# Two batch pairs of a fused retention and adapter kernel: scores as causal 64x64 tiles with a state, or as whole 128x128 chunks

## The chip, the cores and the metric

The kernel runs on one core of one Trainium2 chip. Its time is the device time in microseconds, median of several runs. The engines of the core are TensorE (PE in the profile; PEld is its weight load), VectorE (DVE), ScalarE (ACT), GpSimd (POOL) and SyncE (SP), whose queue issues most DMA transfers. Each engine takes its instructions in program order and waits on semaphores that other engines raise.

## The reference

Eight batches, eight heads, 576 positions, head dimension 64. First a retention layer without softmax, then a mixture of low-rank adapters on its output:

```python
scores = scale * np.matmul(q, k.transpose(0, 1, 3, 2))
gamma = 1.0 - 2.0 ** (-5.0 - np.arange(H, dtype=np.float32))
Dmat = np.where(rel >= 0, gamma[:, None, None] ** rel[None, :, :], 0.0)   # rel = i - j
x = np.matmul(scores * Dmat[None], v)          # B H S D, then to rows of B*S by H*D
...
logits = x @ w_gate                            # 8 experts, the best 2 chosen
w = softmax over the two chosen logits
out = x + sum over the chosen e of w_e * (x @ A[e]) @ B[e]     # rank 16
```

The decay gamma^(i-j) splits into gamma^i on the query and gamma^(-j) on the key, so that a causal 0/1 mask is all that is left to apply to the scores. Since there is no softmax, all earlier positions can be summed into one 64x64 matrix of keys by values for each head, a state; the product of a query with that state stands for all of them.

## The kernel before

The work is cut into 18 units. Units 0 to 15 are (chunk c, batch pair bp): 128 positions of two batches with eight heads each; units 0 to 3 are the first chunk (c = 0) of the four pairs, units 4 to 7 the second, and so on. Units 16 and 17 hold the last 64 positions of four batches each. All work of a unit goes through the same stages:

- `load` brings q, k, v by the SP queue (L182). `scale_` (L210) multiplies keys or queries by their powers of gamma.
- `stage_T` (L234) transposes keys or queries on TensorE with the 64x64 identity; `evict_T` (L285) copies the result from PSUM to `kT` or `qT`.
- scores, sums and products, in one of two forms, below.
- `stage_Z` (L511, called by `logits` and `logits_half`): x times AW, which holds the rank-16 adapters A of all experts (128 columns) and the gate (8 columns). `routing_1` to `routing_4` choose the experts: a ScalarE copy of the logits (`zs`), VectorE maxima (`choose`), ScalarE sigmoid (`routing_3`), GpSimd weighting (`routing_4`).
- `back` (`stage_B`, L574) transposes x back to rows in PSUM, `small` (`stage_P`, `evict_z`) transposes the weighted 128 values and ScalarE copies them to `zT`; `output` (`stage_Y`, `evict_o`) adds zT times B into the same PSUM banks, and ScalarE copies them out to `osb`. `store` writes to memory.

Units 0 to 3 use the whole-chunk form: `first_S` (L426) scores 128 keys against 128 queries of a head pair with unscaled transposes and multiplies them by the full decay table `dec` on VectorE (L442, four instructions a unit); `first_U` (L463) sums keys by values of all 128 positions to the state `SP[bp]` (copy L478); `first_X` (L480) multiplies 128 scores by v. Only the keys are scaled, after their transposes, for the sums.

Units 4 and up use the tiled form, in halves t = 0, 1 of 64 positions: `stage_S` (L316) scores only the two diagonal 64x64 tiles of each head; `masks` (L337) applies the triangle on VectorE (four instructions of 64 partitions), writing into `qT` or the tile `x2`; `stage_U` (L349) sums each half by itself, `stage_A` (L385) adds the first half's sums to the state (`sm`) and then the second's (`SP`). Half t = 0 takes `SP` as its state and half t = 1 takes `sm`. `put_state` (L368) copies a state to the 64 partitions of the v tile that the half does not fill; `shift_q` (L308) copies queries to the facing 64 partitions of `x2`. So `stage_X` (L394) gets scores times v and queries times state in one contraction over 128 rows. From unit 4 on the queries of a full unit are loaded with even and odd positions apart.

PSUM has eight banks, named by tags s0, s1, x0, x1, u0, u1, o0, o1; a stage that writes a bank waits for the last reader of the one before it.

The order of the work is written out by hand. L663 to L735 are units 0 and 1; L946 to L1004 finish unit 1 and take units 2 and 3 and the beginning of unit 4, each interleaved with the routing of earlier units; L1006 on is the rest, in a loop from unit 5. The adapters A arrive as `arow` (32 rows of 2048), are reordered by two GpSimd copies (`sort_A`, L640), transposed by 16 TensorE instructions and copied to AW by VectorE (`place_A`, L645). Transfers of later units start by a count of products: `product` (L158) adds 4 for a float32 product and 2 for a transpose or a 16-bit one, and at each 255th count `feed` lets the SP queue issue the next half round of loads, and, in the last rounds, of stores (`transfers`, L744).

Of the kernel before, what the change touches and what calls it, by code (L numbers as in the profile page):

```python
# [18 lines left out]
def kernel(  # L19
# [49 lines left out]
    pack_np = np.concatenate([id64_np, gk_np[:, 0], tri_np], axis=1).astype(np.float32)  # L69
# [38 lines left out]
    tri = pack[:, 64 + H : NPK]  # L108
# [3 lines left out]
    def factor(w, c):  # L112
        if c == 0:
            return pack[:, 64 : 64 + H]
        return (gk2 if w == "k" else gq2)[:, c - 1, :]
# [16 lines left out]
    def first_chunk(u):  # L132
        return u < NP
# [15 lines left out]
    def block(u, t):  # L149
        return nt(u, "v")[:, t]  # L150
# [31 lines left out]
    def load(u, w, parts=(0, 1), at=None):  # L182
        if u >= NU:
            return
        c, bp = units[u]
        s0 = 128 * c
        if c == NFULL:
            for t in parts:
                hf = slice(64 * t, 64 * t + 64)
                dst = block(u, t)[hf] if w == "v" else nt(u, w)[hf]  # L190
                move(dst, rows(w, 4 * bp + 2 * t, 2, s0, 64), at)
        elif w == "v" and c == 0:
            move(block(u, 0), rows(w, 2 * bp, 2, s0, 128), at)
        elif w == "v":
            for t in parts:
                hf = slice(64 * t, 64 * t + 64)
                move(block(u, t)[hf], rows(w, 2 * bp, 2, s0 + 64 * t, 64), at)
        elif w == "q" and paired(u):
            for b in parts:
                move(  # L200
                    nt(u, w)[64 * b : 64 * b + 64].rearrange("p (h e) d -> p h (e d)", e=2),
                    q[2 * bp + b, :, s0 : s0 + 128, :].rearrange(
                        "h (p e) d -> p h (e d)", e=2
                    ),
                    at,
                )
        else:
            move(nt(u, w), rows(w, 2 * bp, 2, s0, 128), at)
# [76 lines left out]
    def evict_T(u, w, b=None, engines=(nc.scalar, nc.scalar)):  # L285
        tl = transposed(u, w)
        for r, eng in enumerate(engines):
            copy = eng.copy if eng is nc.scalar else eng.tensor_copy
            if w == "k" and first_chunk(u):
# [47 lines left out]
    def masks(u, b=None, order=((0, 0), (1, 0), (0, 1), (1, 1))):  # L337
# [47 lines left out]
    def stage_A(u):  # L385
# [3 lines left out]
        nc.vector.tensor_tensor(out=sm, in0=pu[0], in1=SP[bp], op=ALU.add)  # L389
# [4 lines left out]
    def stage_X(u, tag="x", bs=(0, 1)):  # L394
        px = st[u].setdefault("px", {})
        for b in bs:
            px[b] = pp.tile([128, HP, 2, ST], FP32, tag=f"{tag}{b}", name=f"px{b}")
# [65 lines left out]
    def first_U(u, tag="u0"):  # L463
# [14 lines left out]
        nc.vector.tensor_copy(out=SP[units[u][1]], in_=pu)  # L478
# [161 lines left out]
    def sort_A():  # L640
        rows_ = arow.rearrange("p (d r) -> p r d", r=R)
        for r in (slice(0, R // 2), slice(R // 2, R)):
            nc.gpsimd.tensor_copy(out=asort[:, r], in_=rows_[:, r])

    def place_A(tag):  # L645
        pa = pp.tile([128, R, E * HP], FP32, tag=tag, name="pa")
        for r in range(R):
            product(
                pa[:, r, :], lhsT=asort[:, r, :], rhs=id64[64 : 64 + E * HP, 0 : E * HP],
                is_transpose=True, start=True, stop=True,  # L650
            )
        nc.vector.tensor_copy(  # L652
            out=AW[:, :, 0:ER].rearrange("p t (e r) -> p t e r", e=E),
            in_=pa.rearrange("p r (e t) -> p t e r", t=HP),
        )
# [24 lines left out]
    asort = atile[64 : 64 + E * HP].rearrange("p (r d) -> p r d", r=R)  # L680
# [15 lines left out]
    share = (nc.vector, nc.scalar)  # L696

# [37 lines left out]
    sort_A()  # L735
# [63 lines left out]
    def sums(u):  # L799
        if is_full(u):  # L800
            stage_U(u)
            if units[u][0] > 0:
                stage_A(u)

    def put(u):
        if is_full(u):
            src = st[u]["sm"] if units[u][0] > 0 else st[u]["pu"][0]
            put_state(u, 1, src, nc.scalar)
# [149 lines left out]
    scale_(2, "k", pool2)  # L958
# [124 lines left out]
```

## Time and profile before

| | |
|---|---|
| median of 3 runs | 177.18 us (176.99 to 177.76) |
| the profiled execution: its time | 178.47 us |
| its span, first to last instruction | 176.6 us |
| mean granted TensorE clock | 0.991 |
| read and written in memory | 29.11 MB, 9.44 MB |
| first scores of unit 1 | 16.17 us |
| first logits (unit 0) | 22.73 us |
| scores of unit 4 | 46.60 us |
| last store issued | 172.0 us |

The chain of waits goes back from the last instruction to what released each. The groups give, for each line, engine and shape, the busy time, the mean of one and the idle time before; L159 is the helper that issues every TensorE instruction, so its groups are told apart by tile: `pf_s`, `pf_u`, `pf_x` are scores, sums and products of whole chunks, `ps_s`, `pu`, `px` those of tiles, `pt_k` and `pt_q` the transposes, `pz` and `pzh` the logits, `po` the way back and the output, `pzt` the small transpose, `pa` the adapters. A float32 product is two instructions.

### The profile page before, as it was taken

What the parts mean: (1) busy time and instruction counts of PE and PEld (TensorE: products, weight loads), DVE (VectorE), ACT (ScalarE), POOL (GpSimd) and SP (SyncE); (2) the same over time, 40 slices, a digit from 0 to 9 for tenths busy, and PEclk for the clock granted to TensorE, in tenths of its full rate; (3) what the DMA queues carried; (4) which work ended last, traced back from release to release, by engine and by line L of the source; (5) the groups of instructions that cost most, each with busy time, mean ns of one, the idle gap of its engine ahead of it and who ended that gap; (6) DMA issues with size and microseconds to landing.
All of it is one profiled execution on the core that took longest, in us unless ns stands there. A gap on an engine that the chain in (4) does not pass through costs nothing.

```text
span 176.6 us, 9664 instructions
## 1 busy us (share of the span) xinstructions
PE 167.9 (95%) x4306; PEld 151.7 (86%) x4306; DVE 112.4 (64%) x221; ACT 105.8 (60%) x242; POOL 113.0 (64%) x162
## 2 busy tenths in 40 slices
PE   7999999999999999999999999999999999999950
PEld 7789988888998999999999998989898889898930
DVE  0375626552766978787889878777776765847060
ACT  3225225744677595858677676768586765584730
POOL 1228608697498477959497959696975797930250
PEclk9999999999999999999999999999999999999996
DMA  6989999999964778787878787959679899999994
GB/s 153 270 190 230 243 238 236 246 249 225 249 148 126 173 191 182 187 186 190 196 188 198 187 194 178 227 143 220 164 164 223 183 247 255 377 390 346 348 358 144
DMA packets 105929, 39.04 MB, mean 221 GB/s; under 512 B 88664, under 2 KB 101336, under 8 KB 105856
## 3 DMA queue, kind: packets, MB, share of 16 engines
q1 hardware_dynamic: 105360, 37.64, 83.9%
q8 instruction: 34, 0.56, 1.3%
q0 software_dynamic: 288, 0.52, 1.3%
q10 hardware_dynamic: 240, 0.25, 0.5%
q14 instruction: 7, 0.06, 0.1%
HBM read 29.11 MB, written 9.44 MB: 218 GB/s over the span
## 4 chain that ended last, share of the span: by engine, by line
PE 87%; DVE 5%; ACT 2%; issue 2%; POOL 1%; POOLq 0%; ACTq 0%
PE px L159 17%; PE pz L159 16%; PE ps_s L159 9%; PE po L159 9%; PE pu L159 6%; PE pt_k L159 6%; PE pt_q L159 5%; PE pf_s L159 4%; PE pf_x L159 4%; PE pf L159 3%; PE pf_u L159 2%; DVE qT L347 2%; DVE x L347 2%; PE pzh L159 1%; PE pzt L159 1%
## 5 line engine op out<-in xcount | busy, mean ns | idle before, releaser
L226 POOL TENSOR_TENSOR k<-k,pack 128x512 f32<-128x512 f32 x36 | 38.5, 1087 | 27.6 <-DMA k<-in_k_dram 18.4
L159 PE MATMUL pz<-AW,xT 128*128 128x136 f32 x256 | 34.2, 286 | 0.1
L159 PEld LDWEIGHTS pz<-AW,xT 128*128 128x128 f32 x256 | 30.8, 190 | 1.4 <-DVE AW L652 0.3
L159 PE MATMUL px<-x,v 128*64 128x64 f32 x448 | 30.0, 224 | 0.6 <-issue 0.5
L159 PE MATMUL px<-qT,v 128*64 128x64 f32 x448 | 29.6, 224 | 0.1
L159 PEld LDWEIGHTS px<-x,v 128*64 128x64 f32 x448 | 27.6, 138 | 2.4 <-issue 0.8
L159 PEld LDWEIGHTS px<-qT,v 128*64 128x64 f32 x448 | 27.2, 138 | 0.0
L347 DVE TENSOR_TENSOR x<-ps_s,pack 64x512 f32<-64x512 f32 x28 | 19.3, 689 | 10.8 <-PE ps_s L159 10.4
L216 POOL TENSOR_TENSOR qs<-q,pack 128x512 f32<-128x512 f32 x24 | 24.5, 1043 | 1.8 <-DMA q<-in_q_dram 1.0
L529 ACT COPY zs<-pz 128x272 f32<-128x272 f32 x16 | 6.2, 386 | 25.3 <-PE pz L159 24.0
L374 POOL COPY v<-SP 64x512 f32<-64x512 f32 x32 | 19.5, 611 | 1.6
L347 DVE TENSOR_TENSOR qT<-ps_s,pack 64x512 f32<-64x512 f32 x28 | 19.3, 689 | 0.8
L615 ACT COPY osb<-po 128x512 f32<-128x512 f32 x32 | 17.1, 591 | 2.7 <-PE po L159 2.7
L310 DVE COPY x<-qT 64x512 f32<-64x512 f32 x14 | 10.1, 724 | 13.0 <-ACT qT L294 9.1
L159 PEld LDWEIGHTS ps_s<-qT,kT 64*64 64x64 f32 x896 | 14.7, 134 | 3.3 <-issue 1.3
L159 PE MATMUL ps_s<-qT,kT 64*64 64x64 f32 x896 | 16.9, 221 | 0.1
L554 ACT ACTIVATE sg<-zs,ns 128x8 f32<-128x8 f32 x34 | 8.4, 293 | 13.5 <-DVE ge L544 12.8
L564 POOL TENSOR_TENSOR cm<-ge,sg 128x16 f32<-128x16 f32 x17 | 5.7, 337 | 16.5 <-ACT sg L554 16.5
L374 ACT COPY v<-sm 64x512 f32<-64x512 f32 x24 | 14.9, 620 | 0.1
L299 ACT COPY kT<-pt_k 128x512 f32<-128x512 f32 x28 | 14.8, 579 | 0.2 <-PE pt_k L159 0.2
L566 POOL TENSOR_TENSOR zc<-zs,cm 128x128 f16<-128x128 f32 x34 | 13.6, 421 | 1.3
L159 PE MATMUL pu<-v,k 64*64 64x64 f32 x768 | 14.2, 221 | 0.1
(89 smaller groups left out, 302.0 us busy)
## 6 DMA issues: line engine op xcount, KB each, us to landing
q<-in_q_dram SPq DMA_DIRECT2D x32, 256.0 KB, 4.4
out_dram<-osb SPq DMA_DIRECT2D x32, 256.0 KB, 4.3
k<-in_k_dram SPq DMA_DIRECT2D x14, 512.0 KB, 5.3
v<-in_v_dram SPq DMA_DIRECT2D x28, 256.0 KB, 4.1
k<-in_k_dram SPq DMA_DIRECT2D x8, 256.0 KB, 5.0
v<-in_v_dram SPq DMA_DIRECT2D x4, 512.0 KB, 5.7
q<-in_q_dram SPq DMA_DIRECT2D x2, 512.0 KB, 6.8
arow<-in_moe_A_dram SPq DMA_DIRECT2D x1, 256.0 KB, 4.6
```

The lines of the kernel that those rows point to most:

```text
L159: mm = nc.tensor.matmul(out, lhsT=lhsT, rhs=rhs, is_transpose=is_transpose, **kw)
L216: engines[b].tensor_tensor(out=qs[:, :, 4 * b : 4 * b + 4, :].rearrange("p e h d -> p h e d"), in0=tl[:, b * H : b * H + H, :].rearrange(" ...
L226: engines[b].tensor_tensor(out=tl[:, b * H : b * H + H, :], in0=tl[:, b * H : b * H + H, :], in1=factor(w, c).unsqueeze(2).broadcast_to((1 ...
L299: copy(out=tl[:, r], in_=st[u]["p" + w][r])
L310: eng.tensor_copy(out=x2[64:128, 0, b], in_=qT[0:64, 0, b])
L347: nc.vector.tensor_tensor(out=out, in0=in0, in1=m, op=ALU.mult)
L374: copy(out=dst[:, :, :, ho, :], in_=src[64 * ho : 64 * ho + 64])
L529: nc.scalar.copy(out=zs, in_=s["pz"])
L554: nc.scalar.activation(out=sg[:, b, :], in_=s["zs"][:, b, ER : ER + E], func=AFT.Sigmoid, bias=s["ns"][:, b : b + 1], scale=2.0,)
L564: nc.gpsimd.tensor_tensor(out=cm, in0=s["ge"], in1=s["sg"], op=ALU.mult)
L566: nc.gpsimd.tensor_tensor(out=zc[:, b, :].rearrange("p (e r) -> p e r", e=E), in0=s["zs"][:, b, 0:ER].rearrange("p (e r) -> p e r", e=E), ...
L615: copy(out=s["osb"][:, :, :, ho, :], in_=s["po"][ho])
```

## The change

Units 2 and 3 take the tiled form; only units 0 and 1 stay whole chunks. Having no positions before them, they have no state for t = 0: `stateful(u)` is false for them. Then `stage_X` contracts only 64 rows for t = 0, `stage_A` copies the first half's sums instead of adding, and `masks` does both tiles of t = 0 first. Keys and queries are scaled before the transposes (`mixed` gives one batch to GpSimd and one to VectorE), the table `pack` gets the queries' factors, and v of units 2 and 3 is loaded in two halves. `stage_X` can be called for one half t alone. The adapters A are transposed by four VectorE instructions of 32 partitions each, straight into AW; `sort_A` is gone. The sums of unit 1 are copied by ScalarE. The order of L946 to L1004 is written anew.

```diff
-    pack_np = np.concatenate([id64_np, gk_np[:, 0], tri_np], axis=1).astype(np.float32)
+    pack_np = np.concatenate(
+        [id64_np, gk_np[:, 0], gq_np[:, 0], tri_np], axis=1
+    ).astype(np.float32)
...
-    def first_chunk(u):
-        return u < NP
+    def whole_chunk(u):
+        return u < 2
+
+    def stateful(u):
+        return units[u][0] > 0
...
-        elif w == "v" and c == 0:
+        elif w == "v" and whole_chunk(u):
...
-    def masks(u, b=None, order=((0, 0), (1, 0), (0, 1), (1, 1))):
+    def masks(u, b=None):
+        order = ((0, 0), (1, 0), (0, 1), (1, 1)) if stateful(u) else (
+            (0, 0), (0, 1), (1, 0), (1, 1)
+        )
...
-        nc.vector.tensor_tensor(out=sm, in0=pu[0], in1=SP[bp], op=ALU.add)
+        if stateful(u):
+            nc.vector.tensor_tensor(out=sm, in0=pu[0], in1=SP[bp], op=ALU.add)
+        else:
+            nc.vector.tensor_copy(out=sm, in_=pu[0])
...
-    def stage_X(u, tag="x", bs=(0, 1)):
+    def stage_X(u, tag="x", bs=(0, 1), ts=(0, 1)):
...
-                for t in range(2):
+                for t in ts:
+                    kp = slice(0, 128) if t or stateful(u) else slice(0, 64)
...
-                            lhsT=block(u, t)[:, b * H + 2 * hp + ho, :],
-                            rhs=facing(u, t, ho)[:, b, hp, :],
+                            lhsT=block(u, t)[kp, b * H + 2 * hp + ho, :],
+                            rhs=facing(u, t, ho)[kp, b, hp, :],
...
-    def first_U(u, tag="u0"):
+    def first_U(u, tag="u0", engine=nc.vector):
...
+    def place_A(groups):
+        rows_ = arow.rearrange("p (g d r) -> p g r d", g=4, r=R)
+        for g in groups:
+            nc.vector.transpose(
+                out=AW[32 * g : 32 * g + 32, :, 0:ER].rearrange("p t (e r) -> p r e t", e=E),
+                in_=rows_[:, g],
+            )
...
+    mixed = (nc.gpsimd, nc.vector)
...
+    place_A(range(1))
     first_S(1, 0, "s")
     first_S(1, 1, "o")
-    first_U(1)
+    first_U(1, engine=nc.scalar)
     first_X(1, "x")
-    place_A("u1")
+    place_A(range(1, 4))
     back(0)
+    scale_(2, "k", mixed)
     logits(0, "u1")
+    scale_(2, "q", mixed)
     choose(0)
     routing_3(0)
     routing_4(0)
     stage_T(2, "k", tag="s")
     evict_T(2, "k")
-    scale_(2, "k", pool2)
     stage_Z(1, "u0", (0,))
     stage_T(2, "q", tag="x")
     evict_T(2, "q", engines=share)
     stage_Z(1, "u0", (1,))
+    shift_q(2, nc.vector)
     routing_1(1)
-    small(0, "u1")
     choose(1)
     routing_3(1)
-    first_S(2, 0, "s")
-    first_S(2, 1, "x")
+    scores(2)
+    small(0, "x1")
     output(0)
-    routing_4(1)
-    first_U(2)
+    sums(2)
+    scale_(3, "k", pool2)
+    scale_(3, "q", pool2)
+    put(2)
+    back(1)
+    stage_X(2, ts=(0,))
     stage_T(3, "k", tag="s")
-    evict_T(3, "k")
-    scale_(3, "k", pool2)
-    first_X(2, "x", (0,))
+    evict_T(3, "k", engines=share)
+    stage_X(2, ts=(1,))
+    evict_x(2)
     stage_T(3, "q", tag="u")
     evict_T(3, "q", engines=share)
-    first_X(2, "x", (1,))
-    back(1)
-    small(1, "x0")
-    first_S(3, 0, "s")
-    first_S(3, 1, "x")
+    routing_4(1)
+    small(1, "s0")
+    shift_q(3, nc.vector)
+    logits_half(2, 0, "x0")
+    scores(3)
     output(1)
-    scale_(4, "k", pool2)
-    scale_(4, "q", pool2)
-    first_state(4)
-    for w in "kq":
-        scale_(5, w, pool2)
-    first_U(3)
+    for u in (4, 5):
+        for w in "kq":
+            scale_(u, w, pool2)
+        if u == 4:
+            first_state(4)
+    sums(3)
     seen["round"] = 3
-    logits_half(2, 0, "u1")
-    first_X(3, "x", (0,))
+    put(3)
+    logits_half(2, 1, "x1")
     stage_T(4, "k", tag="o")
     evict_T(4, "k")
-    sums(4)
+    stage_X(3, ts=(0,))
     stage_T(4, "q", tag="s")
     evict_T(4, "q")
-    first_X(3, "x", (1,))
-    logits_half(2, 1, "o0")
-    shift_q(4, nc.vector)
     choose(2)
     routing_3(2)
+    stage_X(3, ts=(1,))
+    evict_x(3)
+    shift_q(4, nc.vector)
+    sums(4)
     put(4)
     routing_4(2)
```

More of the change, by code (lines that the diff above doesn't have):

```diff
@@ L107 @@
     id64 = pack[:, 0:64]
-    tri = pack[:, 64 + H : NPK]
+    tri = pack[:, 64 + 2 * H : NPK]
     fac = cpool.tile([128, 128 + HP * 128], FP32, tag="fac", name="fac", align_bytes=256)
@@ L113, in factor @@
         if c == 0:
-            return pack[:, 64 : 64 + H]
+            return pack[:, 64 : 64 + H] if w == "k" else pack[:, 64 + H : 64 + 2 * H]
         return (gk2 if w == "k" else gq2)[:, c - 1, :]
@@ L288, in evict_T @@
             copy = eng.copy if eng is nc.scalar else eng.tensor_copy
-            if w == "k" and first_chunk(u):
+            if w == "k" and whole_chunk(u):
                 bs = slice(0, 2) if b is None else slice(b, b + 1)
@@ L477, in first_U @@
                     )
-        nc.vector.tensor_copy(out=SP[units[u][1]], in_=pu)
+        copy = engine.copy if engine is nc.scalar else engine.tensor_copy
+        copy(out=SP[units[u][1]], in_=pu)
     def first_X(u, tag, bs=(0, 1)):
@@ L638, in store @@
                     )
[L640 to L650, printed above, removed]
-            )
[L652 to L655, printed above, removed]
+    def place_A(groups):
[4 more added lines that the diff above has]
+                in_=rows_[:, g],
+            )
     def load_batch(u, w, b):
@@ L679 @@
     arow = atile[0 : E * HP]
-    asort = atile[64 : 64 + E * HP].rearrange("p (r d) -> p r d", r=R)
     nc.sync.dma_start(out=arow, in_=moe_A.rearrange("e (t p) r -> (e t) (p r)", t=HP))
@@ L734 @@
     evict_T(1, "q", 1, share)
-    sort_A()
     def prepare(t):
@@ L801, in sums @@
             stage_U(u)
-            if units[u][0] > 0:
-                stage_A(u)
+            stage_A(u)
     def put(u):
         if is_full(u):
-            src = st[u]["sm"] if units[u][0] > 0 else st[u]["pu"][0]
-            put_state(u, 1, src, nc.scalar)
+            put_state(u, 1, st[u]["sm"] if stateful(u) else st[u]["pu"][0], nc.scalar)
     def products(u):
```

3 lines of the change are left out of this document (2 added, 1 removed).

## The prediction, made before the changed kernel ran

> **What bounds the kernel now.** I read the page's engine sums first, then the sums by stretch.
>
> ```profile
> PE 167.9 (95%) x4306; PEld 151.7 (86%) x4306; DVE 112.4 (64%) x221; ACT 105.8 (60%) x242; POOL 113.0 (64%) x162
> 28.50:46.60 18.10, 18.10 (x366) 15.80 (x369) 10.15 (x20) 9.95 (x21) 13.35 (x17) 1.00 1.04 237
> ```
>
> TensorE is busy 95% of the span, and in the stretch that the change rewrites (second row, columns PE, PEld, DVE, ACT, POOL) it is busy 18.10 of 18.10 us; VectorE has 8 us to spare there, ScalarE too. So a matmul removed here is time gained, unless TensorE then waits for an engine that was hidden. The chain of waits gives the price of each stage (start, us, what; x counts instructions, two for a float32 product).
>
> ```profile
> 20.84 1.12 PE pa L159 x16
> 21.99 0.70 DVE AW L652
> 22.73 2.12 PE pz L159 x16
> ...
> 26.62 0.65 PE pt_q L159 x16
> 27.27 1.12 PE pz L159 x8
> 28.39 0.11 PE pzt L159 x2
> 28.50 1.99 PE pf_s L159 x32
> 30.49 0.54 PE po L159 x4
> 31.03 1.08 PE pf_u L159 x32
> ...
> 32.76 1.02 PE pf_x L159 x16
> ...
> 46.60 1.09 PE ps_s L159 x64
> ...
> 51.10 1.08 PE px L159 x32
> 52.18 1.09 PE pu L159 x64
> ```
>
> The rows from 46.60 on are the tiled form, which units 4 to 15 use already. I measure the change from logits(0) (22.73) to the scores of unit 4 (46.60), because both kernels run the same stages between these two, though in another order, and the same program after.
>
> **Term 1, TensorE work.** A whole-chunk unit costs 1.99 + 1.08 + 2 x 1.02 = 5.11 us (scores, sums, products), a tiled one 1.09 + 1.09 + 2 x 1.08 = 4.34. Two units: **-1.54 us**. The products of t=0 contract 64 rows, not 128. No row has that form; at best it runs like the sums (1.09 for 64 instructions, so 0.55 for a half), at worst like px (1.08). Both outputs of a t=0 pair use rows 0 to 63, so half of the array has no work, where the sums alternate between both halves: I take 1.08, the bound being 1.1 us lower for two units.
>
> **Term 2, the weights A.** Removed: two strided GpSimd copies (sort_A), 16 PE transposes (1.12) and one VectorE copy. Added: four VectorE transposes of 32x512.
>
> ```profile
> 17.16 2.48 DVE L442 TENSOR_TENSOR sc<-pf_s,dec 128x512 f32<-128x512 f32 x4 [0.52 <-PE pf_s L159]
> L389 DVE TENSOR_TENSOR sm<-pu,SP 128x512 f32<-128x512 f32 x12 | 8.3, 691 | 5.3 <-PE pu L159 4.9
> L643 POOL COPY arow<-arow x2: 1954/1962/1971, 16.6 to 18.5; 32x1024 f32<-32x1024 f32 x2
> L374 POOL COPY v<-SP 64x512 f32<-64x512 f32 x32 | 19.5, 611 | 1.6
> ```
>
> A has landed by 16.6, where GpSimd begins to copy it. VectorE is free from 17.16 - 0.52 = 16.64; the first transpose goes there, then the four masks of unit 1 (2.48), then the other three. logits(0) needs all four: 16.64 + 2.48 + 4 tau. A VectorE pass over 512 elements takes 0.69 us (L389), the lower end. The transposes read with a step of 16 floats; GpSimd's copy with that step took 1962/1024 = 1.92 ns an element against 611/512 = 1.19 without, a factor of 1.6, which makes 1.11 the upper end. VectorE's copy of A out of PSUM, which reads with a step too, took 0.70 (21.99 above), so I take tau = 0.8, nearer to the lower end: logits(0) at 22.35, **-0.38 us** (-0.8 to +0.85). TensorE gets there at 20.84 + 0.65 (back(0): 16 transposes, as in T) and waits. [...]
>
> The sums of unit 1 are copied by ScalarE instead of VectorE; ScalarE has nothing to do before the products of unit 1 end, so this costs nothing, and VectorE gets its three transposes 0.7 us sooner.
>
> **Term 3, a new wait at output(0).** TensorE now runs T(2,q), Z(1) half, scores(2), small(0), output(0). output(0) needs the ScalarE copy zT, which stands behind the sigmoid of unit 1, which needs choose(1) on VectorE, which stands behind the new shift_q(2).
>
> ```profile
> 27.30 0.69 DVE L299 COPY qT<-pt_q 128x512 f32<-128x512 f32 x1 [1.47 <-PE pt_q L159]
> 27.48 2.04 POOL L226 TENSOR_TENSOR k<-k,pack 128x512 f32<-128x512 f32 x2
> 28.71 0.38 ACT L508 COPY zT<-pzt 128x256 f16<-128x256 f16 x1
> 28.84 0.24 DVE L539 MAX8 m<-zs 128x8 f32<-128x8 f32 x2 [0.86 <-ACT zs L529]
> 29.63 0.49 ACT L554 ACTIVATE sg<-zs,ns 128x8 f32<-128x8 f32 x2 [0.55 <-DVE ge L544]
> L310 DVE COPY x<-qT x14: 420/619/1305, 45.6 to 157.6; 64x512 f32<-64x512 f32 x14
> L311 DVE COPY x<-qT x14: 421/1170/1171, 46.0 to 158.1; 64x512 f32<-64x512 f32 x14
> ```
>
> Today zT (28.71) precedes the sigmoid (29.63). Now, from the end of T(2,q): qT copy 0.69, two shift copies, choose 28.84 to 29.63 = 0.79, sigmoid 0.49, zT 0.38, five handovers of some 0.04: 2.55 without the shifts. Their rows give shortest, median and longest in ns: together 0.84 at least and 2.48 at most; GpSimd scales keys just then (27.48 today, unit 3's keys in the same place after), so I take a mean of 1.6. In all 4.15; TensorE covers 1.12 + 1.09 + 0.11 = 2.32. **Stall 1.8 us** (1.1 to 2.7). Behind output(0) TensorE holds sums(2), back(1) and products(2), all late by it. [...]
>
> The next wait is near: products(2) of t=1 need the four masks, the new sm copy and put(2).
>
> ```profile
> L347 DVE TENSOR_TENSOR x<-ps_s,pack 64x512 f32<-64x512 f32 x28 | 19.3, 689 | 10.8 <-PE ps_s L159 10.4
> L374 ACT COPY v<-sm 64x512 f32<-64x512 f32 x24 | 14.9, 620 | 0.1
> 46.63 0.27 ACT L788 COPY zs<-pzh 128x136 f32<-128x136 f32 x1 [0.53 <-PE pzh L159]
> ```
>
> From the end of choose(1): 4 x 0.69 + 0.69 + 2 x 0.62 + 0.1 = 4.8; TensorE, from the same point: 1.0 to output(0) (sigmoid 0.49, zT 0.38, handovers), then 0.54 + 1.09 + 0.65 + 1.08 + 0.65 = 4.0, in all 5.0. It fits by 0.2: nothing added.
>
> **Term 4, a new wait in products(3).** The second batch of t=0 writes bank x1, which logits_half(2, 1) filled and ScalarE empties behind put(3). From the end of scores(3): masks 2.76, sm 0.69, put 1.24, zs 0.27, handovers 0.15: 5.1. TensorE covers output(1) 0.54, sums(3) 1.09, logits_half 1.12, T(4,k) 0.65, one batch of t=0 0.54: 3.94. **Stall 1.2 us** (1.15 to 1.5, the more if shift_q(3) still holds VectorE). Behind put(3) on ScalarE also stand the copies of kT(4) and qT(4); scores(4) come some 3.3 us after the stall and need 0.3 + 4 x 0.6 of them, so they are covered.
>
> **Edits at nothing.** Keys and queries of units 2 and 3 are scaled before their transposes; four query instructions are new.
>
> ```profile
> 15.66 0.50 SPq L174 DMA_DIRECT2D k<-in_k_dram  x1
> 23.35 2.21 SPq L174 DMA_DIRECT2D q<-in_q_dram  x1
> k<-in_k_dram SPq DMA_DIRECT2D x1, 512.0 KB, 5.5
> q<-in_q_dram SPq DMA_DIRECT2D x1, 512.0 KB, 6.8
> ```
>
> k(2) lands at 15.66 + 5.5 = 21.2. Half goes to GpSimd (1.04, half of the 2.04 above), half to VectorE after the transposes: ready by 23.4, and T(2,k) comes at 24.4. Without that cover the wait would be 1.0. The latest is q(3): 23.35 + 6.8 = 30.15, scaled at 32.2, with routing_4(1) queued behind it until 33.2; small(1) needs that at about 36. k(4) is not in yet then, so no later scaling is pushed. v(2) and v(3) are two DMAs each instead of one, of the same bytes on the same queue. The shared copy of kT(3) on VectorE (0.69) lies after sm, where TensorE has products.
>
> **Term 5, the stores.** Loads and stores start at every 255th count of products (4 for a float32 product, 2 else). Each tiled unit counts 384 instead of 192, the lost transposes 32: +352, one block and 97. All later transfers start 97 counts earlier in the program; the last stores start in the scores of unit 17 instead of back(15), earlier by the logits between them (2.12) and parts of the two, some 3 us.
>
> ```profile
> 164.00:165.00 1.00, 1.00 (x41) 1.00 (x38) 0.00 (x0) 1.00 (x3) 0.76 (x2) 1.00 0.50 182
> DMA to landing us min/median/max: 3.2/3.4/3.5
> pack<-c_pack ACTq DMA_DIRECT2D x1, 100.0 KB, 2.2
> ```
>
> The DMA engines are half idle at 164 (share 0.50, the last column but one), and the final stores (second line, shortest, median and longest us of 128 KB stores) land 3.4 us after issue, behind that queue; a transfer of like size at the very start, with little ahead of it, lands after 2.2 (last row). Starting the stores earlier fills the gap (0.5) and shortens the queue: the gain is between 0 and 3.4 - 2.2 = 1.2. I take **-0.7**, the gap and a little.
>
> **Sum.** -1.54 - 0.38 + 1.8 + 1.2 - 0.7 = +0.4 us. The profiled execution took 178.47 (span 176.6): 178.9. The median of the runs shown is 1.29 lower: 177.18 + 0.4 = **177.6**.
>
> **Rivals.** A measurement of this kernel can tell 0.5%, 0.9 us: under 176.3 is faster, over 178.1 slower.
> - A, slower: the strided transposes. At 1.11 each, logits(0) starts 4 x 0.31 = 1.2 later than forecast: 178.8. It decides from 0.92 each on. For it GpSimd's factor, against it VectorE's 0.70 for today's copy. 0.18. [...]
> - B, slower: the last data, not the store queue, sets the end; term 5 falls away: 178.3. For it: the last stores are issued within 0.5 us of their data. 0.14.
> - C, slower: the change does not shorten TensorE's work, because switching between half and whole contraction costs what the tiles save: 179.1. Against it: units 4 and up pay 1.09 in mixed company. 0.05.
> [...]
> - The forecast, no change that can be told: 0.40.
>
> So faster 0.23, same 0.40, slower 0.37. Likeliest case alone: 176.3 to 178.1. With the bounds of tau (+1.2), the port and the t=0 form, 8 in 10: 176.0 to 179.2.
>
> **What would show it.** Scores and sums of units 2 and 3 at 1.09 us each; logits(0) near 22.35 and the transposes' mean near 0.8 us; TensorE idle some 1.8 us before output(0), ended by ScalarE's zT, and 1.2 us in products(3), ended by zs; scores(4) near 47.7; DMA share near 1 at the end until the last store. It is wrong if there is no idle time at these two places, if the idle time stands elsewhere (put(2) first), or if the tail keeps its length.

## The result, and the profile after

The changed kernel takes 182.88 us, the median of 6 runs (181.81 to 184.29); the kernel before took 177.74 beside it (176.99 to 178.25). The ratio is 1.0301, 95% interval 1.026 to 1.0341: slower, outside the predicted range. The profiled execution took 183.72 us with a span of 181.9, against 178.47 and 176.6 before, so +5.3 us of span are to be explained. (Lines have moved: the product helper is L164, the transposes of A L657.)

The page's engine sums, the row of granted clock in 40 slices, and the instruction queue of its list of DMA queues:

```profile
PE 167.7 (92%) x4482; PEld 151.4 (83%) x4482; DVE 111.7 (61%) x232; ACT 108.6 (60%) x246; POOL 111.1 (61%) x162
PEclk9999999699999999999999999999999999999997
q8 instruction: 35, 0.57, 1.3%
```

TensorE is busy as long as before (167.7 against 167.9 us), though it does less: one slice ran at a lower clock. The rest of the 5.3 us is time in which it stands still. The chain of waits (start, us, what) between the logits of unit 0 and the scores of unit 4, at the places that the prediction named:

```profile
17.93 2.45 DVE sc L455 x4
20.41 1.15 DVE AW L657
21.58 1.15 DVE AW L657
22.73 1.13 DVE AW L657
23.91 2.12 PE pz L164 x16
...
28.48 0.69 DVE qT L304
29.20 0.72 DVE x L315
29.94 1.17 DVE x L316
31.12 0.25 DVE m L553 x2
31.39 0.64 DVE ns L554
32.03 0.10 DVE ge L558
32.12 0.49 ACT sg L568 x2
32.62 0.27 ACT zT L522
...
33.63 1.92 PE pu L164 x64
...
36.59 1.15 PE px L164 x32
...
38.39 1.08 PE px L164 x32
...
47.08 0.28 ACT zs L793
...
50.90 1.14 PE ps_s L164 x64
```

Logits(0) start at 23.91 instead of 22.73 (+1.18), because each transpose of A takes 1.13 to 1.15 us (and the first of the four, ahead of these rows, began at 16.94, when A had landed). From there to the scores of unit 4 it is 26.99 us instead of 23.87 (+3.12). TensorE's timeline (start, us, instruction; in brackets the idle time before it and what ended it) shows the two waits:

```profile
32.93 0.70 PE L164 MATMUL po<-Bcat,zT 128*128 128x256 f16 x4 [2.05 <-ACT zT L522]
47.41 0.27 PE L164 MATMUL px<-x,v 64*64 64x64 f32 x1 [0.98 <-ACT zs L793]
```

Behind the first of them the sums of unit 2 take 1.92 us instead of 1.09. The view by stretches (window, length, busy time and count of PE, PEld, DVE, ACT, POOL, then clock, DMA share, GB/s) says why:

```profile
33.00:34.00 1.00, 1.00 (x20) 0.67 (x24) 0.97 (x3) 0.65 (x2) 0.92 (x4) 0.66 1.21 274
34.00:36.00 2.00, 2.00 (x70) 1.88 (x64) 1.04 (x3) 0.43 (x1) 0.04 (x1) 0.50 0.63 158
36.00:37.00 1.00, 1.00 (x24) 0.88 (x22) 0.90 (x2) 0.65 (x2) 0.68 (x1) 0.64 1.21 310
```

TensorE was granted half its clock from 33.3 to 36.7 us (a mean of 0.66 over the first microsecond means half for 0.68 of it, 0.64 over the last for 0.72). The chain's rows give what that cost: output(0) 0.70 instead of 0.54, the sums 1.92 instead of 1.09, the way back 1.05 for 0.65, the first products 1.15 for 1.08: 1.46 us. So the stretch adds up: 2.05 + 0.98 + 1.46 - 1.54 (the work saved) = 2.95 of the 3.12. The six runs' mean clocks fit: 181.81 us at 0.995, 182.80 to 183.72 at 0.985 to 0.987, 184.29 at 0.976.

From the scores of unit 4 to the end it is 131.0 us instead of 130.0. The end itself is shorter, as the landing of the last stores (shortest, median and longest us, row of the tile `oe`) and the chain show:

```profile
DMA to landing us min/median/max: 2.7/2.9/3.0
```

```profile
172.38 1.00 PE pze L164 x8
```

The same row of the chain before:

```profile
166.08 1.00 PE pze L159 x8
```

From the last logits to the end of the span it is 181.9 - 172.38 = 9.52 us; before it was 176.6 - 166.08 = 10.52. So 1.0 is gained there and 2.0 is lost between. The view of waits (who waits, for whom; us in total, times, longest) names a loss that no term of the prediction has, "issue", time in which TensorE waits for nothing that the profile shows:

```profile
PE po L164 <- ACT zT L522: 2.1, 1, 2.1
PE px L164 <- issue: 1.1, 2, 0.8
PE ps_s L164 <- issue: 0.6, 1, 0.6
PE pz L164 <- issue: 0.5, 1, 0.5
```

The kernel before has one row of that kind, 0.5 us. These halts are what most of the experiments are about.

### The profile page after: what moved, and what is told of

Its sections match the earlier page's. It is cut to its first block, busy times and chain, and to the rows that moved or that the text cites. A ratio compares the mean times of both kernels' runs of the same rounds, so it can differ in the third digit from the quotient of the medians.

```text
span 181.9 us, 10038 instructions
## 1 busy us (share of the span) xinstructions
PE 167.7 (92%) x4482; PEld 151.4 (83%) x4482; DVE 111.7 (61%) x232; ACT 108.6 (60%) x246; POOL 111.1 (61%) x162
## 4 chain that ended last, share of the span: by engine, by line
PE 83%; DVE 9%; issue 3%; ACT 2%; POOL 1%; POOLq 0%; ACTq 0%; DVEq 0%
PE px L164 18%; PE pz L164 18%; PE po L164 9%; PE ps_s L164 9%; PE pu L164 8%; PE pt_k L164 6%; PE pt_q L164 6%; PE pf L164 3%; PE pf_s L164 2%; DVE AW L657 2%; DVE sc L455 1%; PE pf_x L164 1%; DVE x L316 1%; PE pzt L164 1%; DVE x L315 1%
## 5 line engine op out<-in xcount | busy, mean ns | idle before, releaser
L164 PE MATMUL px<-x,v 128*64 128x64 f32 (+1 forms) x512 | 35.1, 224 | 2.1 <-issue 1.1
L164 PE MATMUL pz<-AW,xT 128*128 128x136 f32 x256 | 34.7, 287 | 2.2 <-DVE AW L657 1.7
L164 PEld LDWEIGHTS px<-x,v 128*64 128x64 f32 (+1 forms) x512 | 31.9, 138 | 4.0 <-issue 1.4
L164 PE MATMUL px<-qT,v 128*64 128x64 f32 (+1 forms) x512 | 34.6, 224 | 0.0
L355 DVE TENSOR_TENSOR x<-ps_s,pack 64x512 f32<-64x512 f32 x32 | 22.0, 688 | 20.0 <-PE ps_s L164 19.7
L164 PEld LDWEIGHTS pz<-AW,xT 128*128 128x128 f32 x256 | 30.9, 190 | 3.8 <-DVE AW L657 1.9
L164 PEld LDWEIGHTS px<-qT,v 128*64 128x64 f32 (+1 forms) x512 | 31.5, 138 | 0.3
L355 DVE TENSOR_TENSOR qT<-ps_s,pack 64x512 f32<-64x512 f32 x32 | 22.0, 688 | 0.9
L164 PEld LDWEIGHTS ps_s<-qT,kT 64*64 64x64 f32 x1024 | 17.1, 134 | 4.0 <-issue 2.3
L164 PE MATMUL ps_s<-qT,kT 64*64 64x64 f32 x1024 | 19.5, 222 | 0.7 <-issue 0.6
L304 ACT COPY kT<-pt_k 128x512 f32<-128x512 f32 x31 | 16.6, 587 | 1.7 <-PE pt_k L164 1.7
L164 PE MATMUL pu<-v,k 64*64 64x64 f32 x896 | 17.1, 228 | 0.0
L164 PEld LDWEIGHTS pu<-v,k 64*64 64x64 f32 x896 | 15.1, 141 | 1.7 <-PE po L164 0.3
```

What stands on the lines that cost most here:

```text
L164: mm = nc.tensor.matmul(out, lhsT=lhsT, rhs=rhs, is_transpose=is_transpose, **kw)
L304: copy(out=tl[:, r], in_=st[u]["p" + w][r])
L355: nc.vector.tensor_tensor(out=out, in0=in0, in1=m, op=ALU.mult)
```

## The experiments

Three theories share the loss: the path of A (+1.2 us), the two waits with the half clock behind the first (+4.5 us), and the halts. The rival to the last two is that they are one thing: an idle TensorE and what follows from it. Each edit is of the changed kernel unless said otherwise, and each ratio is to the kernel before on the same chip.

**Does the idle time cause the half clock?** Zero products, into a bank that nobody reads, fill the wait at output(0).

```diff
     small(0, "x1")
+    pf = pp.tile([128, 512], FP32, tag="x0", name="pf")
+    for _ in range(32):
+        nc.tensor.matmul(pf[:, 0:84], lhsT=zero[:, 0:128], rhs=zero[:, 0:84], start=True, ...)
     output(0)
```

> The changed kernel with 32 idle-time products of zeros (some 1.8 us) on TensorE between small(0) and output(0), into a free bank; nothing else moves, and the wait for zT is as long as before. Theory (the idle gap of 2.1 us halves the granted clock for some 3 us afterwards, and the sums of unit 2 take 1.92 instead of 1.09, back(1) 1.05 instead of 0.65): granted clock stays 1.00 from 33 to 37, sums of unit 2 near 1.09, the time 1.2 to 1.5 us lower, near 181.5. Rival (the sums of unit 2 are slow for another reason, such as transfers or operands that arrive late): sums stay near 1.9, the time does not change, or grows where the fill overruns the gap.

188.8 us, ratio 1.0558 (1.045 to 1.0665). TensorE's timeline and its waits:

```profile
31.84 0.61 PE L164 MATMUL po<-Bcat,zT 128*128 128x256 f16 x4 [0.84 <-ACT zT L522]
32.38 1.16 PE L164 MATMUL pu<-v,k 64*64 64x64 f32 x64
```

```profile
PE ps_s L164 <- issue: 2.3, 5, 0.7
```

With 0.84 us idle instead of 2.05 the sums run at full clock. Yet the kernel is slower still: issue, 2.3 us in this row alone, sums to 10.0 us at the places found below, against 3.5 in the changed kernel. The fill was issued past the helper, so the count by which transfers start no longer matches TensorE's instructions. The same fill through the helper:

```diff
-        nc.tensor.matmul(
+        product(
```

> The fill in the gap before output(0) once more, but now the 32 products of zeros count for the transfers like all others. The uncounted fill kept the clock at 1.00 and the sums of unit 2 at 1.09, yet the kernel took 188.8, with pauses of TensorE under issue, 255 instructions or a multiple apart, from there to the end. Theory (the count keeps each burst of transfers just behind the border of a block of some 255 TensorE instructions, where the next block is fetched; uncounted instructions put the bursts on top of the fetch): with the fill counted these pauses fall back to some 2 to 3 us in all, and what is left is the gain of the clock, 1.2 to 1.5 us: near 181.5. Rival (more instructions alone cost it, by their fetch): pauses as many as with the uncounted fill, time over 186.

182.11 us, ratio 1.0218 (1.0159 to 1.0278) instead of 1.0558, by nothing but the place of the transfers; the halts sum to 4.0 us instead of 10.0. The stretch that ran at 0.50:

```profile
34.00:36.00 2.00, 2.00 (x63) 1.86 (x58) 1.47 (x3) 1.13 (x2) 0.86 (x1) 1.00 0.96 264
```

So the idle time brings the half clock here (0.50 from 34 to 36 us behind 2.05 us of it, 1.00 behind 0.84), and the start of the transfers against TensorE's instructions is worth several us (halts of 10.0 us against 4.0).

**The path of A.** The changed kernel with the old path (GpSimd's sorting, 16 TensorE transposes, one copy):

```diff
-    place_A(range(1))
...
-    place_A(range(1, 4))
+    place_A("u1")
```

> The changed kernel with the adapters A brought in as before: two GpSimd copies, 16 TensorE transposes, one VectorE copy. Theory (the four strided VectorE transposes of 1.13 to 1.15 us set the start of logits(0), which stood at 23.91 instead of 22.73): logits(0) back near 22.7, the time about 1.2 us lower, near 181.7; the wait before output(0) stays near 2.1 us. Rival (VectorE's later queue, not the transposes, sets the pace of the whole stretch): logits(0) earlier, but the wait before output(0) or in products(3) grows by as much, and the time moves by less than 0.4 us.

181.13 us, ratio 1.0154 (1.0069 to 1.0239); the logits of unit 0 start at 22.43. By the ratios that is 2.6 us less than the changed kernel where 1.2 was expected, but the interval is 3 us wide. And the kernel before with the new path:

```diff
-    place_A("u1")
+    place_A(range(1, 4))
```

> The kernel before with the four VectorE transposes in place of the copies, TensorE transposes and copy for A; whole chunks for units 2 and 3 as before. Theory: the transposes take 1.13 to 1.15 us each here too, logits(0) starts at 23.8 to 23.9, and with nothing behind it to cover, the time is 1.0 to 1.3 us higher, near 179.2. Rival (the later start is taken up by the slack of the other engines behind it): less than 0.4 us.

182.18 us, ratio 1.0231 (1.0171 to 1.029), from the part that looked like a gain of 0.38. Its chain:

```profile
48.14 1.09 PE ps_s L159 x64
71.45 2.15 issue
```

Logits(0) start at 24.28 (+1.55) and the scores of unit 4 are as late (+1.54), so nothing of a delay at logits(0) is won back; one halt of 2.15 us comes on top. The span is 5.0 us longer than before (181.6 against 176.6), and the trace shows where: 1.54 up to the scores of unit 4; 2.63 from there to the last logits (at 170.25), by the halt and by half the clock from 75.0 to 78.4 us behind it (products at 3.03 instead of 2.02), less some halts that only the kernel before has; and 0.83 behind, 11.35 against 10.52. In that tail the last stores land 4.1 us after their issue instead of 3.4: without 16 transposes the count starts them 32 later in the program.

Why is a transpose that slow? First the reading side: contiguous runs instead of a step of 16 floats (A then stands in another order, so the output differs).

```diff
-        rows_ = arow.rearrange("p (g d r) -> p g r d", g=4, r=R)
+        rows_ = arow.rearrange("p (g r d) -> p g r d", g=4, r=R)
```

> The changed kernel with the four VectorE transposes of A reading 512 contiguous floats instead of every 16th (A's columns land in another order, so the output is not the reference's). Theory (the step of 64 bytes on the reading side costs the transposes 1.13 to 1.15 us instead of some 0.7): 0.65 to 0.75 us each, logits(0) near 22.3. Rival (a 32x32 transpose costs this whatever it reads, or the writing side with its steps sets it): still over 1.0 us each.

VectorE's timeline has the same price, 3.36 for three in a row (3.44 in the changed kernel); the one run took 187.0 us:

```profile
19.85 3.36 DVE L657 STREAM_TRANSPOSE AW<-arow 32x512 f32<-32x512 f32 x3
```

Then the writing side too:

```diff
-                out=AW[32 * g : 32 * g + 32, :, 0:ER].rearrange("p t (e r) -> p r e t", e=E),
+                out=AW[32 * g : 32 * g + 32, :, 0:ER],
```

> After, with the four VectorE transposes reading and writing contiguous runs on both sides (the adapters then stand in AW in another order, so the output differs). If the steps make the transposes slow (reading them alone was excluded by e10_plain_A, so it would be writing): 0.7 us each instead of 1.13. If a transpose of 32x512 has that price by itself: 1.05 to 1.15 each, as before.

```profile
15.83 0.69 DVE L657 STREAM_TRANSPOSE AW<-arow 32x512 f32<-32x512 f32 x1
18.95 2.14 DVE L657 STREAM_TRANSPOSE AW<-arow 32x512 f32<-32x512 f32 x3
```

0.69 to 0.71 each: the write with steps costs some 0.4 us, and the read with steps next to nothing (1.13 to 1.15 with it, 1.10 to 1.12 without) as long as the write has them. A read with steps beside a contiguous write was not run, so what it costs by itself stays open. Logits(0) start at 21.14 here, 2.8 us earlier than in the changed kernel: 1.7 by the four transposes, 1.1 because A had landed earlier (the first transpose starts at 15.83 instead of 16.94). The one run took 181.45 us, where those of the kernel before beside it took 177.61 to 183.82, so its time decides nothing.

**The two waits.** Ahead of put(3), logits_half(2, 1) has its bank emptied in time:

```diff
-    put(3)
     logits_half(2, 1, "x1")
+    put(3)
```

> The changed kernel with logits_half(2, 1) ahead of put(3), so that ScalarE empties bank x1 before the two state copies. Theory (products(3) wait about 1.0 us for zs behind put(3)): that wait is gone and the time about 1.0 us lower, near 181.9. Rival (the wait moves on to the second half of products(3), which needs put(3)): TensorE then waits there, and the time moves by less than 0.4 us.

182.3 us, ratio 1.0213 (1.0127 to 1.03). The wait for `zs` in products(3) is gone, the one for `zT` (2.1 us) stays. That one goes if small(0) runs before scores(2), and choose(1) with its sigmoid behind put(2):

```diff
     routing_1(1)
-    choose(1)
-    routing_3(1)
-    scores(2)
-    small(0, "x1")
+    small(0, "u1")
+    scores(2)
     output(0)
...
     put(2)
+    choose(1)
+    routing_3(1)
```

> The changed kernel with small(0) ahead of scores(2), and choose(1) and the sigmoid of unit 1 behind put(2), so that zT waits for nothing that stands behind shift_q(2). Theory (the order puts zT behind shift_q(2), choose(1) and the sigmoid, 2.1 us of waiting and 1.4 us of half clock): output(0) starts without a wait, the clock stays at 1.00, a smaller wait of some 1.1 us for put(2) shows in the second half of products(2), and the time is 2.0 to 2.6 us lower, near 180.5. Rival (VectorE's masks and sm of unit 2 bound this stretch anyway): the whole wait returns before products(2), the clock falls again, less than 0.7 us gained.

182.36 us, ratio 1.0207 (1.0114 to 1.0301): no wait at output(0) any more, but by the ratios 1.7 us won instead of 2.0 to 2.6, and the intervals overlap; the wait for `zs` grew to 1.3 us. TensorE's timeline and the stretch behind:

```profile
33.81 0.27 PE L164 MATMUL px<-qT,v 64*64 64x64 f32 x1 [0.93 <-issue]
```

```profile
35.00:39.00 4.00, 4.00 (x58) 3.76 (x54) 2.04 (x3) 2.61 (x6) 3.76 (x6) 0.57 0.91 197
```

A halt stands in the products of unit 2 instead, and the half clock (0.57 over these 4 us) follows the halt. All repairs together, and one copy of shifted queries instead of two (units 2 and 3 have no state for t = 0):

```diff
-        eng.tensor_copy(out=x2[64:128, 0, b], in_=qT[0:64, 0, b])
+        if stateful(u):
+            eng.tensor_copy(out=x2[64:128, 0, b], in_=qT[0:64, 0, b])
```

> The changed kernel with all of it at once: A brought in as before, the order at output(0) and in products(3) as in the two runs that changed them, and only the one of the two shift copies that units without a state read. Theory (the tiled form is cheaper, 1.5 us for two units, and the loss is the transposes, the two waits and the half clock behind the first of them): logits(0) near 22.7, scores of unit 4 at or before 46.6, clock 1.00 from 20 to 60, time between 176.5 and 178.5, no longer slower than the kernel before. Rival (two tiled units in this stretch hold up VectorE and TensorE's instruction supply whatever the order): scores of unit 4 still after 48.5, time over 180.

180.21 us, ratio 1.0103 (1.0047 to 1.0158): still 1% slower than before, with every wait of the prediction gone, the tail gain kept (169.36 to 178.9, 9.54 us) and no wait on an engine or a load above 0.4 us in the stretch. The scores of unit 4 start at 47.97, between the marks of the theory (46.6) and of its rival (48.5). What is left, in TensorE's timeline:

```profile
33.20 0.21 PE L164 MATMUL px<-qT,v 64*64 64x64 f32 x1 [0.91 <-issue]
38.73 0.73 PE L164 MATMUL ps_s<-qT,kT 64*64 64x64 f32 x33 [0.47 <-issue]
47.52 0.40 PE L164 MATMUL pu<-v,k 64*64 64x64 f32 x12 [0.68 <-issue]
52.66 0.27 PE L164 MATMUL pzt<-ident,zc 128*128 128x128 f16 x2 [0.56 <-issue]
56.55 0.27 PE L164 MATMUL px<-qT,v 128*64 128x64 f32 x1 [0.26 <-issue]
```

**What the halts are.** They stand at numbers 1197, 1450, 1958, 2213 of TensorE's instructions (loads of weights and products counted together): at a distance of about 255 or a multiple. The page lists one packet of 16 KB on the instruction queue for each 255 instructions (35 for 2 x 4482, 34 before for 2 x 4306). Setting the packets of all 17 profiles against the borders between such blocks, from the instruction and DMA records (a halt here is a gap between two starts over 0.28 us; four borders where `zs` ended the gap are left out; a border without a halt is placed by counting and known to some 0.2 us, so the counts can move by a few):

```
border reached after the packet's end   borders   with a halt
less than 0.95 us                       100       100
0.95 to 1.35 us                          83        32
more than 1.35 us                       353         1

end of the packet to the next start, where there is a halt: median 1.45 us

TensorE took for the 255 before         borders   with a halt
less than 3.6 us                        120        59
3.6 to 4.4 us                           184        54
4.4 to 5.2 us                           160        19
more than 5.2 us                         72         1
```

Where TensorE stood, it went on a median of 1.45 us after the packet had ended. The packet starts a median of 1.2 us behind the previous border where the DMA engines are less than 80% busy around it, and 1.8 us where they are over 95% busy, and takes 1.1. So by these medians a block needs 1.2 + 1.1 + 1.45 = 3.8 us, and 4.4 beside full transfers. That is no minimum: about half of the blocks that TensorE went through in less than 3.6 us had no halt behind them, such as one of 3.3 us in e5_all that ended at 81.9 us, whose packet had started only 0.6 us behind the border. And the tiled form uses blocks up faster: 64 matmul instructions in 1.09 us against 32 in 1.99. The borders in the stretch, in the kernel before, with all repairs, and in a run told next:

```
kernel        border  reached  block took  packet: start after    packet  halt
                                           the border before      ends
before          1197    36.46        6.25  0.50                   31.59   -
                1452    43.00        6.32  0.99                   38.96   -
                1707    47.24        4.19  1.39                   45.63   -
e5_all          1197    32.08        3.25  1.96                   31.86   1.13
                1452    38.04        4.83  2.79                   37.23   0.69
                1962    46.61        3.49  1.65                   46.09   0.90
e11_no_loads    1197    32.15        3.25  2.08                   32.14   1.39
                1452    38.31        4.77  1.21                   35.92   -
```

**Do the transfers delay the packets?** First with units 4 and 5 loaded from contiguous 4 KB runs (other positions, so the output differs). That these take the DMA engines less effort was an estimate of mine that no run had shown.

```diff
-            load(u, w)
+        for w in "kq":
+            move(nt(u, w), plain(w, u, 128))
+        for t in range(2):
+            move(block(u, t)[64 * t : 64 * t + 64], plain("v", u, 64, t))
```

> The kernel with all four mends, but the keys, queries and values of units 4 and 5 are read from contiguous memory, 4 KB a partition in place of rows of 256 or 512 bytes; as many bytes into the same tiles (the values of these units are then other ones, so the output is not the reference's). TensorE's program is the same to the instruction. Theory (the mended kernel's pauses under issue, some 2 us before the scores of unit 4 and 0.8 behind, come from fetches of instruction blocks that queue behind loads, and a tiled unit goes through a block in less time than a fetch then takes): the DMA share between 30 and 45 falls, the pauses there shrink to under 0.7 us in all, scores of unit 4 near 46.0, time 1.3 to 2.5 us below the mended kernel's 180.2. Rival (the pauses belong to the tiled instructions themselves, or to their placement): as many pauses, time within 0.5 of 180.2.

184.42 us, ratio 1.0262 (1.0125 to 1.0399). It did not settle the question, and neither text had it slower: the loads ran at up to 290 GB/s just as early, so the share stayed near 1 up to 42 us (1.01 to 1.05 from 26 us on), and the halts stayed (one of 1.52 us at 32.09). Then without these loads:

```diff
-            load(u, w)
+            nat[(u, w)] = nt(u - 2, w)
```

> e5_all with units 4 and 5 not loaded: they take the keys, queries and values of units 2 and 3 out of their tiles once more, so the output of these two units differs and 3 MB of transfers are missing between 30 and 50 us. Theory (the pauses are blocks of instructions that arrive late behind transfers): the pauses of 0.9, 0.5, 0.7, 0.6 us at 32 to 53 us in e5_all are gone or below 0.3 us each, scores of unit 4 near 46 instead of 47.97, ratio near 0.995. Rival (the tiled form uses a block up faster than the next one can come, whatever else is moved): the same pauses stay, 2 us and more between 30 and 57 us, scores of unit 4 near 48, ratio 1.01.

185.07 us, ratio 1.0345 (1.0259 to 1.043), a time that says nothing of the loads: unit 4's keys now wait for GpSimd in tiles that unit 2 still used, 3.6 us of TensorE waits that the edit itself made. But the first two borders lie ahead of that:

```profile
34.00:38.00 4.00, 4.00 (x91) 3.60 (x91) 2.08 (x5) 3.24 (x8) 3.12 (x6) 1.00 0.02 4
```

```profile
33.54 0.21 PE L164 MATMUL px<-qT,v 64*64 64x64 f32 x1 [1.17 <-issue]
42.54 0.34 PE L164 MATMUL pu<-v,k 64*64 64x64 f32 x8 [2.94 <-POOL k L231]
```

At 33.5, where unit 3's loads still run (a share of 0.50 from 30 to 34 us), the halt is there. At border 1452 (38.3 us) the DMA share is 0.02, the packet came 1.21 us behind the border instead of 2.79, and there is no halt, though the block was used up as fast (4.77 us against 4.83). A milder form holds unit 5's loads back behind chosen products:

```diff
+    load(5, "k", at=seen["at"])
     stage_T(3, "q", tag="u")
...
+    load(5, "q", at=seen["at"])
     logits_half(2, 0, "x0")
...
     scores(3)
+    load(5, "v", at=seen["at"])
```

> e5_all with the loads of unit 5 held back: keys behind the products of unit 2, queries behind the transposes of unit 3's queries, values behind the scores of unit 3, instead of as soon as their tiles are free. Theory (packets late behind transfers): the instruction packets at 36 and 41 us start nearer to the last border (1.1 to 1.5 us behind it instead of 2.8 and 2.0), the pause at 38 us (0.47 in e5_all) goes, the one at 32 stays because its load traffic is that of units 3 and 4; time 0.3 to 1 us below e5_all. Rival (the block is used up too quickly): pauses within 0.3 us of those of e5_all.

181.97 us, ratio 1.008 (1.0034 to 1.0127). As the theory had it, the packet of border 1452 starts earlier, 1.88 us behind the border before (1.1 to 1.5 was expected), and the halt at 38 us is gone. But the halts of all borders sum to 7.6 us, 6.2 in e5_all, and the ratio is not to be told from e5_all's 1.0103. That what is not loaded there is loaded later, beside other packets, is the likely reason and was not tested.

**The place of the transfers.** The kernel before with FIRST = 93, so that its transfers start 97 counts earlier, as the prediction's last term thought of them:

```diff
-    BLOCK, FIRST = 255, 190
+    BLOCK, FIRST = 255, 93
```

> The kernel before with one number changed: the count at which transfers begin, 190, is 93, so that every later load and store starts 97 counts earlier in the program. Theory of the prediction's term 5 (earlier stores leave less of a queue at the end): the last stores land sooner, time about 0.7 us lower. Rival (the same count places the bursts against the borders of TensorE's instruction blocks, and 97 counts off they meet the fetches): pauses of TensorE under issue grow by several us, time 2 to 8 us higher.

No ratio: the four runs lie between 183.58 and 193.74. Even the lowest is 5.7 us above the kernel before beside it (177.93), with the same work for every engine. The theory's own sign is there: in the traced execution (186.49 us) the last stores land 2.8 us after their issue instead of 3.4. Its waits, of which the first two:

```profile
PE pu L159 <- issue: 2.6, 4, 1.0
PE px L159 <- issue: 2.0, 4, 0.9
```

With 190, a burst of transfers is released 13 instructions behind a border, with 93 it is 84 ahead of one. The packets start a median of 1.9 us behind the border instead of 1.3, and there are 12 halts instead of 4. Two runs of e5_all shift the bursts the other way (their labels are crossed: the run named 215 has FIRST = 250, and the other 215).

> e5_all with FIRST = 250 instead of 190: each burst of transfers starts 73 instructions behind the border of a block of TensorE's instructions, not 13. If the packet is asked for at the border, bursts that start later cannot stand ahead of it: lag from border to packet 1.1 us or less in the middle of the loop and no more pauses there than before; the pauses at 32 to 53 us stay, since the loads of units 4 and 5 are not tied to the count. If only the distance to the next border counts, later bursts give more pauses, as FIRST = 93 did: time above 182.

> e5_all with FIRST = 215: bursts start 38 instructions behind the border. Between e5_all and the run with 250: the same theory expects lag and pauses as in e5_all or fewer, time 179.5 to 180.5; the rival 181 and more.

250 gives 189.66 us, ratio 1.051 (1.0448 to 1.0572), with 16 halts of 15.3 us; 215 gives 184.82, ratio 1.0238 (1.0187 to 1.0289). My theory said that a burst behind the request for the packet cannot delay it, and it fell: later bursts are worse too, and with 250 the packets start a median of 1.8 us behind the border, not 1.1 or less. That transfers delay the packets is shown (no loads: 1.21 us behind the border instead of 2.79; loads held back: 1.88; transfers moved by 97 counts: a median of 1.9 instead of 1.3); which moment of a burst does it is not.

## Why the prediction was wrong, point by point

- **Term 1** held: scores, sums and products of units 2 and 3 take 1.09, 1.09 and 1.08 at full clock, products of t = 0 included (1.08 in e2_warm_fill, from 34.11 to 35.19). So rival C is out, but the 1.54 us saved are instructions that run more densely, not fewer: 8612 became 8964.
- **Term 2** failed in its size: 1.13 to 1.15 us a transpose instead of 0.8, logits(0) 23.91 instead of 22.35. Of these 1.56 us some 1.35 are the transposes; most of the rest is that A landed at 16.94, where I had read 16.6 out of the kernel before. I priced the step of the read, and took VectorE's copy at 0.70 as proof that it is cheap. Next to a write with steps it costs 0.03; the price is on the side that I left out, the write with steps (1.10 against 0.69). What the read costs beside a contiguous write no run can tell. Rival A had the price, 1.11 each, for the wrong side; it makes a fifth of the loss.
- **Term 3** was right: 2.05 us for 1.8 (1.1 to 2.7), by the chain foretold (the two shift copies took 0.72 and 1.17 us, 1.6 together was taken), and put(2) was no wait. No run shows the port that the range counts on; what the runs show is that of the shift copies of the kernel before, the three with no GpSimd instruction beside them took 0.42 us each, and the eight of L311 that began inside GpSimd's scaling of keys (L226) 1.17 each, like the second one here. What failed is its price: a wait was taken for its own length, and the half clock behind it (1.46 us in the profiled run) was left out. The profile before had nothing to show it, since TensorE never stood for 2 us in the middle of it, but a bound was missing.
- **Term 4** was right but for its length: 0.98 us, a little under its 1.2 (1.15 to 1.5), ended by `zs`. Without it the ratio is 1.0213 instead of 1.0301 (e3_zs_first), though the intervals overlap.
- **Term 5** was right in what it foresaw, 1.0 us of tail for 0.7 (so rival B is out). The other runs bear it out: with the transfers 32 counts later (e8_before_new_A) the last stores land after 4.1 us, with 97 earlier (e7_before_phase) after 2.8. It was wrong in taking a shift of transfers for a free choice.
- **The frame** failed: "the same program after" the scores of unit 4. No term of the sum stands for TensorE's supply with instructions. The same instructions lost 2.0 us before the tail, because packets of instructions now come later to some borders, where they meet the loads otherwise. By the border count the halts went from 1.7 us to 3.5. The sum for the changed kernel, +1.18 + 2.05 + 0.98 + 1.46 - 1.54 + 1.8 - 1.0 = 4.9, leaves 0.4 of the 5.3 unexplained. For e5_all it is -0.06 (logits at 22.67) - 1.54 + 4.4 (halts, 6.15 against 1.73) - 1.0 = 1.8 of the 2.3 us of its span.

With no more halts than the kernel before, e5_all would come near 176, an estimate from this sum (180.2 - 4.4); no version that I ran was faster than the kernel before, and a looser mixture of dense and sparse stages in units 2 and 3 wasn't tried.

## What to carry to other kernels

Count instructions as well as their time: where TensorE uses up 255 of them in less than some 4 us, it can outrun its own supply (59 of 120 blocks under 3.6 us, 54 of 184 up to 4.4), and what smaller tiles save may be lost again there. A stall in the middle of a dense stretch is to be priced with the clock that may halve behind it (1.46 us here, behind 2.05 of idle time), and a release of transfers tied to instruction counts is a setting that any change of the count can spoil (halts of 10.0 us with 32 products left out of the count, 4.0 with them in it). For a strided instruction, price each side by itself (here 1.10 us with steps in the write alone, 0.69 with none).

## What was not expected of the hardware

- TensorE's supply with instructions is a path of its own: it stood at 100 of 100 borders that it reached less than 0.95 us after the packet's end, and at 1 of 353 that it reached more than 1.35 us after.
- Idle time of 2.05 us ahead of 33 us, and of 0.93 in e4_output0, was followed by half a clock for one stretch of some 3.4 us; 2.3 us at 22 to 24 us in e8_before_new_A and 0.91 in e5_all were not. The length of one gap does not decide. Up to the tail, each trace's records of the granted clock change only in steps of 3.41 us (half for 3.41 or 6.83, full for 27.31 and other multiples), and cut into such slots the 17 traces say more: all 7 full-clock slots in which TensorE was busy for less than 45% were followed by half a clock, and 2 of the other 798 (at 56% and, in e4_output0, 73%). The 2.05 us fell into one slot (40% busy); the 2.3 us were split between two, the first 48% busy. Why the two exceptions fell, and e5_all at 73% did not, stays open.
- A 32x512 float32 transpose on VectorE takes 0.69 us with contiguous sides and 1.10 when only its write has steps of 136 and 16 floats.
